# A new order of the dense work units among the attention units of a one-core transformer block

## The chip, the cores and the metric

One core of a Trainium2 chip. The time is that of the device for one execution, in microseconds (us). Engines: PE is TensorE's matmul row in the profile and PEld its weight loads, DVE is VectorE, ACT is ScalarE, SP issues the DMAs.

## The reference, cut to what matters

```python
def reference(A_x, A_wqkv, A_wo, B_x, B_w1, B_b1, B_w2, B_b2):   # bf16; S=2048, D=1024, 32 heads of 32, F=3584
    xn = layernorm(A_x)
    q, k, v = split_heads(xn @ A_wqkv)
    s = merge(softmax(q @ k.T * 32**-0.5) @ v) @ A_wo            # attention
    y = layernorm(xn)
    g = silu(gelu(y @ B_w1 + B_b1) @ B_w2 + B_b2)                # MLP, tanh form of gelu
    return A_x + s * g
```

## The kernel before

The kernel runs 512 attention units. A unit is four heads, 256 queries and 256 keys. In each turn of the main loop TensorE computes the scores of unit u, then one "dense" unit of other work, then softmax-V and row sums of unit u-1. ACT meanwhile computes the two exponentials of unit u. So dense work fills the time in which TensorE would wait for ACT.

```python
        while u < NU + LAG or state["qi"] < total or dq or act_tasks or due:
            ...
            if u < NU:
                s_unit(u)            # 8 matmuls, row tiles of 32, into 4 banks
            fill_act(u)              # tanhs that are ready may go in front of the exponentials
            if u < NU:
                exp_unit(u)          # 2 exponentials of 128x1024; the scores of u+1 reuse the banks
            ...
                else:
                    pace[:] = pg.lists["tensor"][-1:]
                    for _ in range(1 + (len(due) > 3)):     # one or two loads per unit
                        run_due()
                    pace.clear()
                if entry:
                    for s in it.steps[lo:hi]:               # the dense unit: 8 steps of 4 matmuls, or a piece of W2
                        s(state["bank"])
                    if hi == len(it.steps):
                        it.finish(state["bank"])            # DVE takes the result from the only dense bank
                if state["qi"] == q_end:                    # after the last Q/K/V unit xnT is free
                    for h in range(HG):
                        soon(NPC + 2 * h, ("wo", h), load_wo, h)
                    for t in range(NTB):
                        soon(NPC + 16, ("xres", t), load_xres, t)
                        soon(NPC + 16, ("gres", t), load_gres, t)   # transposing DMA of the gate
            if NP <= u < NU + LAG:
                pv_unit(u - LAG)     # 16 matmuls, column tiles of 32
```

A string lists the dense units in order: `a` is a W1 unit (28 per chunk of tokens, six chunks; two of them share one tanh on ACT), `q` a Q or K projection, `v` a V projection, `w3` one W2 item of 28 steps cut into 3 pieces over 3 units, `o` an output-projection unit, `.` an empty unit. Chunks have 352, 352, 320, 352, 352 and 320 tokens. Weights of W1 and W2 come from HBM anew for each chunk, in loads of 256 KB that wait in the list `due`. Two things are called gates: the gate of an output unit is g of the reference, by which DVE multiplies that unit, and the gates of W1 are the DVE steps that write the tile hT, which W2 reads.

The softmax here doesn't subtract the row's maximum and nothing guards it: scores larger than these inputs give would overflow.

Of the kernel before, what the change touches and what calls it, by code (L numbers as in the profile page):

```python
# [10 lines left out]
I32 = mybir.dt.int32  # L11

PLAN = """
q a a v a a a . a v a v a v a a a q a q a q a v q v a a a a q a a q a a q a v a q a q a q v a a q w3 w4 w3 w4 v w4 w2 w2 w2 a a v a q v v a q q a a a a a q a q a a q a a v a q a v a q a a q a a a q a a v a a q q v a a w3 q w4 w4 v w3 v q v w2 w3 w3 v w4 a v v a q q q a a a a q a a a q a a q v q a a a a v q a q a q a a a v a a q a q v q a v q a v a q a q q a w3 w3 q q q v w5 q v w4 q w3 w4 w4 w2 a a a v v a a a a q a q q v a a q a v q a q a a a a q a a a a a a q v a a a a v a v q a v q q w3 w4 w4 q w4 w4 v v w4 w3 w4 a a q q q a a a v a v a a a a a a v q a a v a a a a a a a v a q q q a a a a q q v q a v v a q w3 q w4 w4 q w4 w4 w4 w4 w4 a a a a q q a a q a a q a a a q a q a q a a a a a q a a a q a q a a a a a a q w2 w4 w3 w4 o w3 o o o o w4 o o o o o o o o o o o o w3 o o o o o o o o o o o o o w4 o o o o o o o o o o o o o . o o . o o o
"""

ENGS = ("sync", "gpsimd", "tensor", "vector", "scalar")
# [1015 lines left out]
```

## Time and profile before

The median was 1100.58 us (1100.17 to 1102.41, 3 runs).

The first part of the page of the kernel before gives busy time, its share of the span, and the number of instructions:

```profile
PE 1079.8 (98%) x29114; PEld 701.5 (64%) x29114; DVE 630.4 (57%) x1413; ACT 1043.8 (95%) x1192; POOL 20.1 (2%) x63
```

Two engines look full, so the shares do not say which one limits, and where. What tells more here is the time from one score group to the next, 503 periods from unit 8 to unit 511, sorted by the dense unit between them. The commonest values in the trace:

```
dense unit               columns streamed   period, us   period minus columns/2.4 per ns
a, q, o of 352 columns        8 x 352         2.073          0.900
a, q, o of 320 columns        8 x 320         1.966          0.899
v                             8 x 256         1.753          0.900   (smallest; median 1.781)
7-step piece of W2, 352       7 x 352         1.923          0.896
14-step piece of W2, 352     14 x 352         2.968          0.914
```

The 2.4 columns per ns are the slope of this table: 0.107 us less for 8 x 32 columns fewer, 0.320 us less for 8 x 96 fewer. At this rate the 0.90 us hold 0.64 us of columns for scores and softmax-V; the rest lies at two changes of tiling. From score start to dense start it is 0.327 us for 0.213 us of columns, and from softmax-V start to the next scores 0.542 for 0.427: 0.11 us per change. The trace does not show what the 0.11 us are made of. With these floors the 503 periods should take 1012.4 us. They took 1028.4. Only these 16 us can be won by an order.

The costs on ACT are in the groups of the kernel before (line, engine, operation, shapes, count | busy us, mean ns | idle before, with its releaser):

```profile
L858 ACT ACTIVATE P<-ps 128x1024 bf16<-128x1024 f32 x1024 | 970.3, 1077 | 16.2 <-PE ps L846 10.8
...
L846 PE MATMUL ps<-QT,KT 32*128 32x256 bf16 x4096 | 203.4, 273 | 7.4 <-ACT P L858 4.4
...
L564 ACT ACTIVATE u<-u 128x704 f32<-128x704 f32 (+1 forms) x84 | 71.0, 848 | 0.0
```

From start to start an exponential takes mostly 0.904 or 0.921 us, so a unit takes about 1.82 us of ACT. With a tanh of 704 columns between, 1.584 us pass: the tanh costs 0.68 (one of 640 columns 0.627). A V unit (1.75 us of TensorE) is shorter than the 1.82 us, and W1 units bring half a tanh each (2.16 against 2.07). There a backlog grows on ACT, and the next scores wait for their banks.

This is how it looks in the timeline of the kernel before, at a V unit whose scores started at 68.85 us (start, duration, what, [idle before and releaser]):

```profile
69.18 1.06 PE L394 MATMUL ps<-wq,xnT 128*32 128x256 bf16 x32
69.33 0.81 ACT L564 ACTIVATE u<-u 128x704 f32<-128x704 f32 x1
...
70.01 1.96 ACT L858 ACTIVATE P<-ps 128x1024 bf16<-128x1024 f32 x2
...
70.39 0.28 PE L878 MATMUL ps<-P,ones 128*32 128x256 bf16 x4
...
71.11 0.40 PE L846 MATMUL ps<-QT,KT 32*128 32x256 bf16 x8 [0.44 <-ACT P L858]
```

The tanh went first, the exponentials began at 70.01, and the next scores started at 71.11 instead of 70.60: a period of 2.26 us instead of 1.75.

The second loss sits at 960 to 990 us, where the output weights, residuals and gates load together with W2 weights. The windows view (stretch; length, then busy us and count for each engine, granted clock, DMA share, GB/s):

```profile
950.00:960.00 10.00, 10.00 (x296) 6.62 (x284) 4.38 (x12) 9.71 (x13) 0.00 (x0) 1.00 0.66 188
960.00:970.00 10.00, 10.00 (x292) 6.70 (x288) 2.09 (x4) 9.96 (x13) 0.00 (x0) 1.00 0.87 267
970.00:980.00 10.00, 8.11 (x224) 4.92 (x220) 3.37 (x8) 9.02 (x11) 0.00 (x0) 1.00 0.96 247
980.00:990.00 10.00, 9.88 (x264) 6.48 (x268) 3.02 (x8) 8.09 (x10) 0.00 (x0) 1.00 1.08 269
```

TensorE is busy for only 8.11 of the 10 us from 970. Two stops make that up. The weight loads of the first one, and the timeline of the second:

```profile
970.29 0.80 PEld L394 LDWEIGHTS ps<-hT,war 128*32 128x32 bf16 x28 [0.21 <-issue]
972.47 0.13 PEld L875 LDWEIGHTS ps<-P,VP 128*32 128x32 bf16 x4 [1.38 <-DVE trs L898]
```

```profile
978.79 0.40 PE L846 MATMUL ps<-QT,KT 32*128 32x256 bf16 x8
979.13 1.29 SPq L636 DMA_TRANSPOSE xnT<-gT_scratch  x1
979.53 0.53 DVE L665 TENSOR_TENSOR wq<-ps,xnT 128x352 f32<-128x352 f32 x1 [1.32 <-DMA xnT<-gT_scratch]
...
980.11 0.26 PEld L394 LDWEIGHTS ps<-hT,war 128*32 128x32 bf16 x12 [1.21 <-DVE wq L665]
```

The second is plain: the first output unit is finished, but DVE cannot multiply it by the gate before the gate's load lands. The only dense bank stays taken, and the next W2 piece waits. The first is put down to DVE by the view, but that transpose had ended at 971.58, and the exponentials that the softmax-V needs at 970.70. It waits for nothing that the program asks for.

### The profile page before, as it was taken

The numbers are of one execution on the slowest core, as the hardware profiler recorded it, in microseconds if no ns is written. First come the engines' busy times: TensorE is split into PE (matmuls) and PEld (weight loads), VectorE is DVE, ScalarE is ACT, GpSimd is POOL, SyncE is SP. The second block draws the span as 40 slices with busy tenths as digits, with TensorE's granted clock in tenths as the row PEclk, the third lists the DMA queues.
The fourth block names the chain that finished last, engine by engine and source line by source line (L and its number), as shares of the span: only waits on it lengthen the run. The fifth ranks groups of instructions, "written<-read, shape, count | busy, mean of one in ns | idle before, by whom it ended". The sixth has DMA issues, their size and how long they took to land.

```text
span 1099.4 us, 61736 instructions
## 1 busy us (share of the span) xinstructions
PE 1079.8 (98%) x29114; PEld 701.5 (64%) x29114; DVE 630.4 (57%) x1413; ACT 1043.8 (95%) x1192; POOL 20.1 (2%) x63
## 2 busy tenths in 40 slices
PE   7999999999999999999999999999999999999998
PEld 5766666666666666666666666666666666666665
DVE  8478853477742477642277843378732477625546
ACT  5799999899998999999999999999999999989994
POOL 2400000000000000000000000000000000000000
PEclk8999999999999999999999999999999999999999
DMA  7844447323373224342433345434244325495433
GB/s 230 164 136 148 131 112 197 92 80 109 90 179 96 72 80 132 94 103 79 132 88 118 107 100 150 119 89 127 62 114 134 90 80 147 130 263 114 105 99 108
DMA packets 209192, 131.92 MB, mean 120 GB/s; under 512 B 52522, under 2 KB 199978, under 8 KB 208938
## 3 DMA queue, kind: packets, MB, share of 16 engines
q1 hardware_dynamic: 208938, 127.97, 42.6%
q8 instruction: 228, 3.74, 1.4%
q14 instruction: 26, 0.21, 0.1%
HBM read 104.87 MB, written 12.06 MB: 106 GB/s over the span
## 4 chain that ended last, share of the span: by engine, by line
PE 54%; ACT 43%; DMA 1%; DVE 1%; SPq 0%; issue 0%; DVEq 0%
ACT P L858 39%; PE ps L394 32%; PE ps L846 9%; PE ps L875 5%; PE ps L878 5%; ACT u L564 4%; PE ps L682 1%; PE ps L698 1%; DMA xnT<-gT_scratch 0%; SPq L623 0%; ACT thz L608 0%; DMA OT<-in_A_x_dram 0%; DVE stats L322 0%; PE ps L385 0%; DVE wq L665 0%
## 5 line engine op out<-in xcount | busy, mean ns | idle before, releaser
L858 ACT ACTIVATE P<-ps 128x1024 bf16<-128x1024 f32 x1024 | 970.3, 1077 | 16.2 <-PE ps L846 10.8
L875 PE MATMUL ps<-P,VP 128*32 128x256 bf16 x4096 | 256.8, 273 | 1.3 <-ACT P L858 1.3
L878 PE MATMUL ps<-P,ones 128*32 128x256 bf16 x4096 | 256.7, 273 | 0.0
L394 PE MATMUL ps<-hT,war 128*32 128x352 bf16 (+1 forms) x5376 | 225.5, 309 | 1.0 <-DVE wq L665 0.9
L394 PE MATMUL ps<-yTc,war 128*32 128x352 bf16 (+1 forms) x5376 | 225.6, 309 | 0.2 <-issue 0.2
L846 PE MATMUL ps<-QT,KT 32*128 32x256 bf16 x4096 | 203.4, 273 | 7.4 <-ACT P L858 4.4
L394 PEld LDWEIGHTS ps<-hT,war 128*32 128x32 bf16 x5376 | 127.9, 96 | 75.4 <-issue 26.9
L394 PEld LDWEIGHTS ps<-yTc,war 128*32 128x32 bf16 x5376 | 127.6, 96 | 74.7 <-DVE xb L547 17.9
L604 DVE TENSOR_SCALAR zh<-ps,b2h 128x352 f32<-128x352 f32 (+1 forms) x48 | 27.5, 572 | 192.8 <-PE ps L394 192.8
L846 PEld LDWEIGHTS ps<-QT,KT 32*128 32x128 bf16 x4096 | 60.7, 92 | 120.2 <-issue 64.5
L547 DVE TENSOR_SCALAR xb<-ps,b1T 128x352 f32<-128x352 f32 (+1 forms) x168 | 96.2, 572 | 51.5 <-PE ps L394 47.5
L875 PEld LDWEIGHTS ps<-P,VP 128*32 128x32 bf16 x4096 | 109.8, 97 | 22.9 <-issue 1.5
L878 PEld LDWEIGHTS ps<-P,ones 128*32 128x32 bf16 x4096 | 109.9, 97 | 18.3
L570 DVE SCALAR_TENSOR_TENSOR hT<-u,xb 128x352 bf16<-128x352 f32 (+1 forms) x168 | 84.4, 509 | 63.3 <-ACT u L564 63.2
L394 PE MATMUL ps<-xnT,wq 128*32 128x352 bf16 (+1 forms) x2688 | 112.6, 309 | 0.0
L394 PEld LDWEIGHTS ps<-xnT,wq 128*32 128x32 bf16 x2688 | 63.8, 96 | 37.1 <-DVE xb L547 10.1
L557 DVE SCALAR_TENSOR_TENSOR u<-u,xb 128x352 f32<-128x352 f32 (+1 forms) x168 | 82.6, 509 | 1.6
L553 DVE TENSOR_TENSOR u<-xb 128x352 f32<-128x352 f32 (+1 forms) x168 | 82.4, 508 | 0.7
L564 ACT ACTIVATE u<-u 128x704 f32<-128x704 f32 (+1 forms) x84 | 71.0, 848 | 0.0
L394 PE MATMUL ps<-xnT,OT 128*32 128x352 bf16 (+1 forms) x1536 | 63.2, 309 | 0.2 <-DVE wq L665 0.2
L890 DVE COPY accs<-ps 128x256 f32<-128x256 f32 x64 | 26.9, 420 | 41.9 <-PE ps L878 41.8
L394 PE MATMUL ps<-wq,xnT 128*32 128x256 bf16 x1536 | 50.8, 274 | 0.0
(52 smaller groups left out, 488.4 us busy)
## 6 DMA issues: line engine op xcount, KB each, us to landing
war<-in_B_w_dram SPq DMA_DIRECT2D x336, 256.0 KB, 3.4
wq<-in_A_wqkv_dram SPq DMA_DIRECT2D x36, 128.0 KB, 2.8
OT<-in_A_x_dram SPq DMA_DIRECT2D x16, 256.0 KB, 5.2
xnT<-in_A_x_dram SPq DMA_DIRECT2D x16, 256.0 KB, 3.8
out_dram<-wq SPq DMA_DIRECT2D x16, 256.0 KB, 2.3
y_scratch<-OT SPq DMA_DIRECT2D x14, 256.0 KB, 2.5
gT_scratch<-gst SPq DMA_DIRECT2D x32, 88.0 KB, 3.2
xnT<-in_A_wo_dram SPq DMA_DIRECT2D x8, 256.0 KB, 4.5
```

What stands on the lines that cost most here:

```text
L394: ins = e.matmul(outs(j), lhsT=lhs(j), rhs=rhs, start=start, stop=stop, tile_position=(0, 32 * j), skip_group_check=True)
L547: x0 = op("vector", lambda e: e.tensor_scalar(xb[:, 0:n], bank(bk, 0, n), b1T[:, f:f + 1], None, op0=ALU.add), r=[("b", bk), "b1"], w=[kx] ...
L553: x = op("vector", lambda e: e.tensor_tensor(ub[:, 0:n], xb[:, 0:n], xb[:, 0:n], op=ALU.mult), r=[kx], w=[ku], c=151 + 1.042 * n)
L557: x = op("vector", lambda e: e.scalar_tensor_tensor(ub[:, 0:n], ub[:, 0:n], 1.0 / 0.044715, xb[:, 0:n], op0=ALU.add, op1=ALU.mult), r=[kx, ...
L564: x = op("scalar", lambda e: e.activation(ut[:, :, 0:n], ut[:, :, 0:n], ACT.Tanh, scale=0.7978845608028654 * 0.044715), r=kus, w=kus, c=48 ...
L570: op("vector", lambda e: e.scalar_tensor_tensor(hT[:, fq, 0:n], ut[:, i, 0:n], 1.0, xq[:, 0:n], op0=ALU.add, op1=ALU.mult), r=[kus[i], kq] ...
L604: x0 = op("vector", lambda e: e.tensor_scalar(zh[:, 0:n], bank(bk, 0, n), 0.25, b2h[:, nb:nb + 1], op0=ALU.mult, op1=ALU.add), r=[("b", bk ...
L846: ins = e.matmul(bank(bks[j], kh * 256, (kh + 1) * 256), lhsT=KT[i2][32 * j:32 * j + 32, k0:k0 + 128], rhs=QT[i2][32 * j:32 * j + 32, qb * ...
L858: op("scalar", lambda e, p=p, sl=sl: e.activation(pb[:, 2 * p:2 * p + 2, :, :].rearrange("p a b q -> p (a b q)"), ps[:, sl * 1024:(sl + 1) ...
L875: e.matmul(bankq(ACC, j, 0, QW), lhsT=VP[vp][:, kb, vo + 32 * j:vo + 32 * j + 32], rhs=pb[:, j, kh, :], start=first, stop=False, tile_posi ...
L878: ins = e.matmul(bankq(ACC, j, QW, 2 * QW), lhsT=ones[:, 0:32], rhs=pb[:, j, kh, :], start=False, stop=last, tile_position=(0, 32 * j), sk ...
L890: op("vector", lambda e: e.tensor_copy(a[:], bank(ACC, 0, QW)), r=[("b", ACC)], w=[ka], c=425.0)
```

## The change

Its intent, as I read it: the same units in another order, so that the tanhs of W1 meet fewer V units, and the loads of the last third are spread. Nothing else changes.

```diff
 PLAN = """
-q a a v a a a . a v a v a v a a a q a q a q a v q v a a a a q a a q a a q a v a q a q a q v a a q w3 w4 w3 w4 v w4 w2 w2 w2 a a v a q v v a q q a a a a a q a q a a q a a v a q a v a q a a q a a a q a a v a a q q v a a w3 q w4 w4 v w3 v q v w2 w3 w3 v w4 a v v a q q q a a a a q a a a q a a q v q a a a a v q a q a q a a a v a a q a q v q a v q a v a q a q q a w3 w3 q q q v w5 q v w4 q w3 w4 w4 w2 a a a v v a a a a q a q q v a a q a v q a q a a a a q a a a a a a q v a a a a v a v q a v q q w3 w4 w4 q w4 w4 v v w4 w3 w4 a a q q q a a a v a v a a a a a a v q a a v a a a a a a a v a q q q a a a a q q v q a v v a q w3 q w4 w4 q w4 w4 w4 w4 w4 a a a a q q a a q a a q a a a q a q a q a a a a a q a a a q a q a a q a a a a a a q w2 w4 w3 w4 o w3 o o o o w4 o o o o o o o o o o o o w3 o o o o o o o o o o o o o w4 o o o o o o o o o o o o o . o o . o o o
+q a a a a q a a q a q v a a a q q a a v v a a a v v a a a a a a a q v a a q v a a a a q q q w2 q v w4 w4 w2 w2 q v w2 q w4 w4 a a a a a q q a v q a a a a a v v q a q a a v a q q a v a a a a v a q a q q v a a a a a a w2 v w4 q w4 w2 w4 w4 w4 w3 a v a q a a v q q q a q v a q a a v a a q q a a q a q a v q a a a v v a a a a q q q v a q a a q a q a q v a v a q a w3 w4 q q q w4 w3 v w4 w3 w4 w3 q v a v v a a a v a a a v q a a a a q v a a v v q a a v q a a v q a a a q a q a a a v q a a a q a w3 w4 w4 w4 w4 q v q q w4 w4 w3 a a a v a q a a a q a q a q a a a v a a a a q a a v a a v q a q a a q a a q q q v v a v a a w2 q v w4 q w5 w3 q q w4 w4 w4 a a a a a q a a q a a a a a a q a q a a a q a a a q q a a q a q a a a a a w2 w4 w3 w4 w3 o o o o o o o o o o w4 o o o o o o o o o o o o w4 o o w4 o o o o o o o o o o o o o o o o o o o o o o . o o .
 """
```

Both strings hold 168 `a`, 84 `q`, 48 `v`, 48 `o` and 48 W2 items. W2 is cut into 167 instead of 166 pieces, and the empty unit near the start is gone. The last `q` is unit 439 of the dense list before and 433 after; the first `o` is 453 before and 455 after.

More of the change, by code (lines that the diff above doesn't have):

```diff
@@ L13 @@
 PLAN = """
-q a a v a a a . a v a v a v a a a q a q a q a v q v a a a a q a a q a a q a v a q a q a q v a a q w3 w4 w3 w4 v w4 w2 w2 w2 a a v a q v v a q q a a a a a q a q a a q a a v a q a v a q a a q a a a q a a v a a q q v a a w3 q w4 w4 v w3 v q v w2 w3 w3 v w4 a v v a q q q a a a a q a a a q a a q v q a a a a v q a q a q a a a v a a q a q v q a v q a v a q a q q a w3 w3 q q q v w5 q v w4 q w3 w4 w4 w2 a a a v v a a a a q a q q v a a q a v q a q a a a a q a a a a a a q v a a a a v a v q a v q q w3 w4 w4 q w4 w4 v v w4 w3 w4 a a q q q a a a v a v a a a a a a v q a a v a a a a a a a v a q q q a a a a q q v q a v v a q w3 q w4 w4 q w4 w4 w4 w4 w4 a a a a q q a a q a a q a a a q a q a q a a a a a q a a a q a q a a a a a a q w2 w4 w3 w4 o w3 o o o o w4 o o o o o o o o o o o o w3 o o o o o o o o o o o o o w4 o o o o o o o o o o o o o . o o . o o o
+q a a a a q a a q a q v a a a q q a a v v a a a v v a a a a a a a q v a a q v a a a a q q q w2 q v w4 w4 w2 w2 q v w2 q w4 w4 a a a a a q q a v q a a a a a v v q a q a a v a q q a v a a a a v a q a q q v a a a a a a w2 v w4 q w4 w2 w4 w4 w4 w3 a v a q a a v q q q a q v a q a a v a q q a a q a q a v q a a a v v a a a a q q q v a q a a q a q a q v a v a q a w3 w4 q q q w4 w3 v w4 w3 w4 w3 q v a v v a a a v a a a v q a a a a q v a a v v q a a v q a a v q a a a q a q a a a v q a a a q a w3 w4 w4 w4 w4 q v q q w4 w4 w3 a a a v a q a a a q a q a q a a a v a a a a q a a v a a v q a q a a q a a q q q v v a v a a w2 q v w4 w4 q w5 w3 q q w4 w4 w4 a a a a a q a a q a a a a a a q a q a a a q a a a q q a a q a q a a a a a w2 w4 w3 w4 w3 o o o o o o o o o o w4 o o o o o o o o o o o o w4 o o w4 o o o o o o o o o o o o o o o o o o o o o o . o o .
 """
```

## The prediction

> **What bounds the kernel now.** TensorE. The page has PE busy 98% and ACT 95% of 1099.4 us[...], so I took the start-to-start times of the 512 score groups (line 846) from the trace. Between two of them lie the softmax-V matmuls of the unit before and one dense unit. The commonest period is 2.073 us for a W1, projection or output unit of 352 columns, 1.966 for 320, 1.75 for a V unit, 1.92 for a 7-step and 2.97 for a 14-step W2 piece: each time the columns at 2.4 per ns plus 0.90 us for scores, softmax-V and two changes of tiling. The two exponentials of a unit take 1.82 us of ACT, less than 2.07; but a paired W1 tanh adds 0.68 us (exp to exp around it 1.58, not 0.90), so runs of W1 units, and W1 beside V units, turn ACT-bound.
>
> From unit 8 to 511 the periods sum to 1028.4 us; the PE floors explain about 1013. Only the excess can be won:
> - about 10 us of exponentials behind tanhs. Adding ACT work against PE floors in program order, with the durations above (an estimate), reproduces all but 14 of 503 periods within 0.06 us.
> - about 3.5 us in the burst at 960 to 990 us (DMA share 0.87 to 1.08 in the windows view): PE stops 1.2 us at 971 with no unmet dependency to be seen while its instruction fetches come late, 1.0 us at 979 because the first output unit's bank waits for the transposed gate load, and less elsewhere.
> - about 1 us of single stops.
>
> **What the change does.** It removes no work: 168 W1, 84 Q/K, 48 V, 48 output units and 48 W2 items stay, W2 in 167 pieces instead of 166; an empty unit goes. In the built program only places move. Prologue (53 us to unit 8) and tail (11 output units, 18 us after unit 511) stay.
> 1. V and Q/K units stand better between W1 units. The same sum over the new order gives an ACT excess of 4.7 us instead of 9.8: minus 5.1, mostly at V units (3.5 to 0.8).
> 2. The last Q/K/V unit comes six units earlier and the first output unit two later: 21 instead of 13 units for the loads of output weights, residuals and gates. I expect 2 to 3 of the 3.5 us back.
> 3. Against it: three chunks now go from the last W1 unit straight into a 14-step W2 piece (the one such place before had a unit between and lost 0.1 us). PE may wait there for the last gates; plus 0.3 us in all.
>
> PE being the limit, all of it is on the critical path: 1100.6 - 5.1 - 2.5 + 0.3 = about 1093.3 us; range 1090.0 to 1098.0. Faster by over 2%: 0.01; within 2%: 0.98; slower: 0.01.
>
> **What would show it.** Busy times within 1% on every engine; median periods unchanged; V units' mean period 1.84 to about 1.77; in the windows view no 10 us stretch in the last 150 us with a DMA share over 0.9, and no PE stop over 0.5 us there; waits for hT small.
>
> **What would make it wrong.** Late gates after the direct W1-to-W2 steps costing 1 to 2 us each; loads newly colliding in W2 phases, so that weights or instructions come late; score groups held by a wait that my sum leaves out.

## The result

The changed kernel took 1095.05 us (median of 4 runs, 1093.9 to 1096.37) against 1100.38 us (4 runs) beside it. The ratio is 0.995, with a 95% interval of 0.9932 to 0.9968. A later repetition gave 1094.68 us and 0.9951 (0.9937 to 0.9964).

The same lines of the page after, the busy times and the three groups:

```profile
PE 1078.7 (99%) x29114; PEld 701.8 (64%) x29114; DVE 631.4 (58%) x1413; ACT 1041.6 (95%) x1192; POOL 20.1 (2%) x63
```

```profile
L858 ACT ACTIVATE P<-ps 128x1024 bf16<-128x1024 f32 x1024 | 968.4, 1079 | 10.4 <-PE ps L846 5.4
...
L846 PE MATMUL ps<-QT,KT 32*128 32x256 bf16 x4096 | 203.3, 273 | 3.1 <-ACT P L858 0.6
...
L564 ACT ACTIVATE u<-u 128x704 f32<-128x704 f32 (+1 forms) x84 | 71.3, 853 | 0.0
```

The work is the same to 0.3%. What fell is idle time: that of PE before the scores from 7.4 to 3.1 us, that of ACT before the exponentials from 16.2 to 10.4. The waits view alone would mislead: "PEld ps L846 <- ACT P L858" is 55.3 us in 204 waits before and 52.9 us in 217 after, because the weight-load row is idle some 0.2 us ahead of nearly all scores (before, 305 more such waits, 64.5 us in all, are put down to "issue") and the view puts this down to whatever came last.

The 503 periods give the split. They took 1028.4 us before and 1022.6 after. I cut each period at the start of its dense unit and at the start of its softmax-V, and summed what lies above the usual length of each of the three parts (us, profiled executions; the last two are experiments below):

```
                          before   changed   changed, again   e1     e2
ahead of the dense unit     1.0      0.2         0.3          1.9    0.1
in the dense unit           2.5      1.4         2.0          0.9    0.4
ahead of the next scores   11.1      8.6         7.1          7.2   10.9
  of these at V units       4.2      1.2         1.2          1.3    4.1
```

The first row before was the late gate (of the 1.9 us of e1, 0.7 us are a stop of another kind). The third is mostly the wait for ACT; in the first execution of the changed kernel 1.5 us of it are stops of that other kind, shown below. So ACT waits fell from about 11 to about 7 us, of which 3 us at V units: their mean period fell from 1.841 to 1.783 us. The gate wait of 1 us is gone. But the other stops stayed. The windows view after:

```profile
940.00:950.00 10.00, 9.24 (x260) 6.02 (x254) 7.14 (x16) 9.07 (x12) 0.00 (x0) 1.00 0.80 235
950.00:960.00 10.00, 10.00 (x292) 6.66 (x288) 2.90 (x7) 10.00 (x12) 0.00 (x0) 1.00 0.87 231
960.00:970.00 10.00, 9.38 (x268) 5.93 (x261) 2.90 (x7) 8.95 (x11) 0.00 (x0) 1.00 1.01 253
970.00:980.00 10.00, 10.00 (x292) 6.73 (x292) 2.43 (x5) 9.94 (x13) 0.00 (x0) 1.00 0.94 229
```

The burst is longer and begins earlier, but it is hardly thinner: two loads are released per unit as soon as more than three wait, whatever the deadline. The timeline after, at the stop in the first of these stretches:

```profile
948.19 0.28 PE L878 MATMUL ps<-P,ones 128*32 128x256 bf16 x4
948.19 0.10 PEld L875 LDWEIGHTS ps<-P,VP 128*32 128x32 bf16 x1
...
949.12 0.29 PE L875 MATMUL ps<-P,VP 128*32 128x256 bf16 x4 [0.65 <-issue]
949.12 0.10 PEld L875 LDWEIGHTS ps<-P,VP 128*32 128x32 bf16 x3 [0.83 <-issue]
```

TensorE stopped between the first and the second of four equal weight loads of one group. No semaphore lies between them: the view says "issue". The unexplained stop of before turns out to be of the same kind. The page shows a DMA queue that it calls "instruction":

```profile
q8 instruction: 228, 3.74, 1.5%
```

228 packets of 16,384 bytes for 58,397 records of TensorE: one packet per 256 records. If TensorE's records are numbered in order of time, the stops at 972.40 us before and at 111.93, 949.12 and 963.46 us after all stand at a number that leaves 193 when divided by 256, which I call a block start. (The traces do not explain the offset of 193 itself.) There are 228 block starts too, so I pair packets and block starts in order of time; the packet of a block is called its fetch. At the four stops the packet was late: it began 2.42 to 2.46 us before TensorE went on. In quiet stretches (before, 860 to 940 us; after, 840 to 930) the packet begins with a median of 0.5 to 0.7 us after the preceding block start; in the burst of the changed kernel the median was 1.9 us, and 2.7 and 3.0 us at the two stops of 0.8 us (0.92 us less the 0.1 that lies between matmuls anyway). At the stop of before it was 3.3 us.

In these two executions (440 block starts from 54 to 1075 us) the packet began 2.40 us or more after the preceding block start in nine cases, and in all nine TensorE's records have a gap at the block start, of 0.28 to 1.27 us. Of the other 431 block starts, whose packets began at most 2.28 us after the preceding one, two have a gap of 0.24 us or more: 0.24 us at 560.81 before, which the view puts down to ACT, and 0.32 us at 102.12 after. Away from block starts these two traces have no gap of that size that the view puts down to "issue". Over all executions the border is less sharp: a few starts at 2.4 to 2.6 us had no stop, and one at 2.05 us had one.

The traces show when a packet begins, not when it was asked for, so they do not show why it was late. What they do show is that late packets and dense loads come together. For this I took all 14 profiled executions and sorted their 3088 block starts (54 to 1075 us) by the DMA share in the first 2 us of the preceding block: below 0.2 the packet begins a median of 0.3 us after the preceding block start, and none of 1129 block starts has a stop (0.24 us or more from one record to the next, with no semaphore as cause); at 0.8 and above the medians are 1.1 to 1.2 us and 30 of 533 have one, of 42 in all. Six of the 42 came at a share below 0.6, so the share does not tell everything.

### The profile page after: what moved, and what is told of

The parts are those of the page before. It is cut to its first block, busy times and chain, and to the rows that moved or that the text cites. A ratio compares the mean times of both kernels' runs of the same rounds, so it can differ in the third digit from the quotient of the medians.

```text
span 1093.2 us, 61739 instructions
## 1 busy us (share of the span) xinstructions
PE 1078.7 (99%) x29114; PEld 701.8 (64%) x29114; DVE 631.4 (58%) x1413; ACT 1041.6 (95%) x1192; POOL 20.1 (2%) x63
## 4 chain that ended last, share of the span: by engine, by line
PE 59%; ACT 40%; DVE 1%; issue 0%; DMA 0%
ACT P L858 36%; PE ps L394 35%; PE ps L846 9%; PE ps L875 6%; PE ps L878 6%; ACT u L564 3%; PE ps L682 1%; PE ps L698 1%; ACT thz L608 0%; DMA OT<-in_A_x_dram 0%; DVE stats L322 0%; ACT xnT L388 0%; PE ps L385 0%; DVE wq L665 0%; ACT VP L702 0%
## 5 line engine op out<-in xcount | busy, mean ns | idle before, releaser
L858 ACT ACTIVATE P<-ps 128x1024 bf16<-128x1024 f32 x1024 | 968.4, 1079 | 10.4 <-PE ps L846 5.4
L846 PE MATMUL ps<-QT,KT 32*128 32x256 bf16 x4096 | 203.3, 273 | 3.1 <-ACT P L858 0.6
L846 PEld LDWEIGHTS ps<-QT,KT 32*128 32x128 bf16 x4096 | 60.6, 92 | 115.0 <-issue 61.5
L394 PEld LDWEIGHTS ps<-xnT,OT 128*32 128x32 bf16 x1536 | 37.5, 96 | 19.9 <-DVE wq L665 7.7
```

The costliest lines, as they stand in the source:

```text
L394: ins = e.matmul(outs(j), lhsT=lhs(j), rhs=rhs, start=start, stop=stop, tile_position=(0, 32 * j), skip_group_check=True)
L846: ins = e.matmul(bank(bks[j], kh * 256, (kh + 1) * 256), lhsT=KT[i2][32 * j:32 * j + 32, k0:k0 + 128], rhs=QT[i2][32 * j:32 * j + 32, qb * ...
L858: op("scalar", lambda e, p=p, sl=sl: e.activation(pb[:, 2 * p:2 * p + 2, :, :].rearrange("p a b q -> p (a b q)"), ps[:, sl * 1024:(sl + 1) ...
```

## The experiments

Two pairs of theories. A: the gain is ACT backlog at V, Q/K and W1 units. B: it is the spread loads. C: the stops without a cause go with late fetches, and these with dense loads of the kernel itself. D: they are waits for data.

### e1 and e2: the new order in one part only

```diff
 # e1: first 323 dense units in the new order, the rest in the old one; e2: the reverse
-PLAN = old
+PLAN = new[units 0..322] + old[units 323..]      # e1
+PLAN = old[units 0..322] + new[units 323..]      # e2
```

At that place both orders have used up the same numbers of each kind of unit, so the halves fit.

> The new order for the first 323 dense units only, the old order after that, so the loads of the last third lie as in the kernel before. Theory A (the gain is ACT backlog that W1 tanhs no longer leave at V and Q/K units): the sum of ACT work against PE floors gives 4.9 us less for the first 323 units and nothing after, so about 1095.5 us, ratio 0.9955. Theory B (the gain is the spread loads of the last third): no gain, 1100.4 us, ratio 1.000.

> The mirror image: the old order for the first 323 units, the new one after. Theory A: the ACT excess stays at 9.6 us against 9.8, and only the stop for the first output gate (about 1 us) goes, so 1099.0 to 1100 us, ratio 0.999. Theory B: nearly the whole gain, 1095.5 us, ratio 0.9955. If A holds, this gain and that of the run before add up to that of the full change (5.3 us).

Measured: e1 1095.64 us, ratio 0.9959 (0.9947 to 0.9971); e2 1098.45 us, ratio 0.9990 (0.9977 to 1.0004), both beside 1100.25. e1 has four fifths of the gain without touching the last third, so A holds and B falls as the main cause. e2 is a small gain that its interval does not clear of zero (by its median 1.8 us, but one of its six times is 1102.41). The two shortfalls, 0.41% and 0.10%, add up to the 0.5% of the whole change. The table above shows the mechanism too: e1 takes 2.9 us off at V units and keeps the late gate (0.9 us at the same W2 piece), e2 keeps the V units and loses the gate wait.

### e3 and e4: shorter tanhs in both orders

```diff
-e.activation(ut[:, :, 0:n], ut[:, :, 0:n], ACT.Tanh, ...)
+e.activation(ut[:, :, 0:16], ut[:, :, 0:16], ACT.Tanh, ...)     # result wrong on purpose
```

> The kernel before with each W1 tanh cut to 32 of its 704 columns (the result is wrong on purpose); order of every instruction unchanged. The cost of one on ACT should fall from 0.68 to about 0.12 us (estimate: the columns' share). Theory A: the ACT excess falls from 9.8 to 1.8 us, so about 1092.4 us. Theory B: ACT is not in the way and the time stays within 2 us of 1100.4.

> The changed kernel with the same cut (wrong on purpose). Theory A: the excess falls from 4.7 to 0.2 us, so about 1090.6 us, and the distance between the two orders shrinks from 5.3 to about 2 us: 1.6 of the empty unit and V units, the rest loads. Theory B: the distance stays near 5 us.

The 0.12 us can be worked out from the two tanhs of the kernel before: 0.680 us for 704 columns and 0.627 for 640 make 0.83 ns per column, which takes 0.56 us off for 672 columns.

Measured: e3 1091.01 us (0.9917), e4 1087.19 us (0.9886), relative errors of 0.03 as intended. A tanh then cost 0.23 to 0.25 us on ACT, not 0.12. The kernel before gained 9.2 us, where A expects 8. But the distance between the orders fell only to 3.8 us, between what A and B expected, and the changed kernel gained 7.5 to 7.9 us (against its two medians) where I had expected 4.5. The traces say why the pair is not clean. The part ahead of the next scores fell from 11.1 to 2.0 us and from 7 to 0.6 us, so the backlog is real in both and I had put it 1 to 2 us too low. With ACT out of the way the old order showed new waits: about 2 us ahead of the dense unit, where DVE had not yet emptied the bank (0.3 in e4), beside one stop of 0.6 us there that waits for no semaphore, and it kept 2.0 us of stops in the dense unit (0.6 in e4). Taking one limit away shows the next one, so this pair supports A but does not measure it.

### e5 and e6: extra copies, bunched and spread

```diff
+dum = nc.dram_tensor("dum_scratch", (8 * 128, 1024), BF16).ap()
+            for i in range(8 if u in (335, 345, 400, 410, 420) else 0):                        # e5
+            for i in range(u % 8, u % 8 + (335 <= u < 355 or 400 <= u < 420)):                # e6
+                op("sync", lambda e, i=i: e.dma_start(dum[128*i:128*i+128, :], B_w1[128*i:128*i+128, 0:1024]),
+                   w=[("dum", i)], dma=f"dum{i}", after=pg.lists["tensor"][-1:])
```

Left out here: the cost that the scheduler books for a copy, and the program's wait for the copies at its very end.

> The changed kernel plus 40 copies of 256 KB from W1 to a scratch tensor that nothing reads: eight at once at units 335, 345, 400, 410 and 420, where DMA was 0.3 to 0.4 busy. Theory C [...]: each burst lasts some 8 us and so holds one or two fetches; these come over 2.2 us late and TensorE stops at the first instruction of a block, place 193 modulo 256 in the order of its records, 0.3 to 1.2 us each, 2 to 6 us in all, with no semaphore as cause. Rival D (the stops are waits for data of the loads): no stop at those places, time unchanged within 1 us, since nobody waits for these copies; at most waits for weights at other places.

> The same 40 copies, one per unit at units 335 to 354 and 400 to 419. Theory C: fetches are late by 1 us at most, no stop over 0.3 us there, time within 1 us of the changed kernel (about 1095 us). Rival D: the same. If it is slower by as much as the bursts, the bytes cost and not their bunching, and theory C falls.

The 8 us of a burst are an estimate: 2.1 MB at the 267 GB/s that the kernel before moved from 960 to 970 us.

Measured: e5 1114.13 us (ratio 1.0117), e6 1094.57 us (0.9944). The same 40 copies cost 19 us when bunched and nothing when spread: not the bytes cost, but their bunching. But the 19 us are not mainly what C expected. Weight loads in e5 (lines are numbered one higher than before), first a stop of kind C, then a wait of the dense unit, with SP's issues ahead of it:

```profile
748.14 0.86 PEld L395 LDWEIGHTS ps<-yTc,war 128*32 128x32 bf16 x25 [0.21 <-DVE xb L548]
750.92 0.12 PEld L395 LDWEIGHTS ps<-yTc,war 128*32 128x32 bf16 x7 [1.92 <-issue]
```

```profile
875.58 3.16 SPq L942 DMA_DIRECT2D dum_scratch<-in_B_w_dram  x5
878.78 2.71 SPq L503 DMA_DIRECT2D war<-in_B_w_dram  x4
```

```profile
879.02 0.39 PEld L395 LDWEIGHTS ps<-yTc,war 128*32 128x32 bf16 x16 [0.21 <-DVE xb L548]
883.97 0.14 PEld L395 LDWEIGHTS ps<-yTc,war 128*32 128x32 bf16 x8 [4.55 <-DMA war<-in_B_w_dram]
```

At 750.92 TensorE stopped for 2.0 us inside one dense unit, at a block start, though nobody reads these copies: that is C. (It lies after 25 of 32 weight loads that come in steps of four, so inside a step, and its packet had begun 4.5 us after the preceding block start.) The larger losses are weights that stood behind the copies, at units 340, 413 and 423, which D allowed for at other places: 11.7 us in six waits of the waits view. And after the two longest waits (4.6 and 4.3 us) the granted clock of the trace is 0.5 for 6.8 us each, from 881.9 and 909.2 us, and the units that followed ran slower by about 3.5 us in all (from 884.88 us four weight loads of softmax-V take 0.16 us, against 0.11 at 878). I had expected one or two stops of kind C in each burst and found one clear one in five. So a stop as C has it does come with a burst, but here the burst hurt data more: 11.7 us of waits for weights, against 2.0 us.

### e7, e10 and e11: moving the blocks under the program

```diff
             for i in range(9):
                 ins = e.matmul(bank(0), lhsT=ident[:], rhs=cold, start=True, stop=True, skip_group_check=True)
+            for i in range(64):      # e11: 32
+                ins = e.matmul(bank(0, 0, 32), lhsT=ident[:, 0:128], rhs=ident[:, 0:32], start=True, stop=True, skip_group_check=True)
             return ins
```

> The changed kernel with 64 more tiny matmuls (128 more instructions of TensorE) in the warm-up at the start, where TensorE is idle, so all later instructions move by half a block of 256. Theory C: every stop without a semaphore as cause now sits at place 193 + 128 = 65 modulo 256, and stops move to other times. Rival D: stops stay at the units where they were, at the same places in the program, whatever the block.

> The kernel of the shift run again, timed, since it had no large stop in the burst and one time of 1092.3 us. My expectation there named the wrong place: the blocks are counted from the first instruction, so they stay at 193 modulo 256 in the records, and it is the program that moves under them by 128; the one stop of that run stood at 193. If the lucky position of blocks against the burst is a lasting property of a build, the median is 1092 to 1093.5 us; if it is chance of each run, 1095 us like the changed kernel.

> The same with 32 tiny matmuls (64 instructions). Stops again only at 193 modulo 256 of the records. The time lies between 1092 and 1096 us; the spread between the three positions (0, 64 and 128 instructions) shows what position alone is worth, by theory C up to 2 us; a rival that knows only of data waits expects no difference over 0.5 us.

Measured: e7 1092.34 us in a single run, state unknown; e10, the same kernel timed, 1093.8 us (0.9939, 0.9926 to 0.9951); e11 1094.56 us (0.9947, 0.9935 to 0.9959). The expectation of e7 named the wrong place, as e10's says: the number 193 stayed and the program moved under it. The gap of 0.52 us in e7, those of 0.54 and 0.57 us in e10 and those of 0.76 and 0.43 us in e11 (each with the usual 0.1 in it) all stand at 193 and wait for no semaphore. The last one has even the same number, 51393, as the one at 963.46 us in the changed kernel, 64 instructions earlier in the program. A wait for data would have moved with the program. What the position is worth in time stays open: the three intervals overlap.

### e8: fewer loads per unit, and what it broke

```diff
-                    for _ in range(1 + (len(due) > 3)):
+                    for _ in range(1 + (len(due) > 3 and (u < 440 or u % 2 == 0))):
```

> The changed kernel with 1.5 instead of 2 loads released per unit from unit 440 on while more than three wait; order of all TensorE work unchanged. Theory C: the DMA share from 940 to 980 us falls from 0.8 to 1.0 to about 0.75, the two stops of 0.82 us there shrink to under 0.4 together, so 1 us less, 1094 us; unless loads forced at their last moment make new waits for weights, which would show as waits of the dense matmuls outside place 193. Rival D: unchanged or slower.

Measured: 1099.43 us, ratio 0.9988 (0.9974 to 1.0002): 4 us worse than the changed kernel. Up to 977 us all went as C says: DMA share 0.56 to 0.77, the latest fetch 1.3 us after its block start, no stop. But the loads now ran late. The waits view of e8:

```profile
PEld ps L394 <- DVE wq L665: 12.3, 37, 4.3
...
DVE wq L665 <- DMA xnT<-gT_scratch: 4.6, 1, 4.6
```

DVE waited 4.6 us for a gate, and the dense bank was held for that time: TensorE lost 4.0 us at the output unit that came next. It is the late gate of the kernel before, made worse. After it the granted clock is 0.5 for 3.4 us, which fits the further 1.4 us that this unit and the next lost (four matmuls of softmax-V take 0.44 us there, against 0.28 at 977). And the stops at block starts came back later: two, of 0.4 us each, at 999 and 1005 us.

### e9: fewer loads per unit, in order of their deadlines

```diff
-                        soon(NPC + 2 * h, ("wo", h), load_wo, h)
+                        soon(NPC - 1.5, ("wo", h), load_wo, h)
-                        soon(NPC + 16, ("xres", t), load_xres, t)
-                        soon(NPC + 16, ("gres", t), load_gres, t)
+                        soon(NPC - 1.4 + 0.01 * t, ("xres", t), load_xres, t)
+                        soon(NPC - 1.4 + 0.01 * t, ("gres", t), load_gres, t)
```

This stands on top of e8's edit. The last group of W2 weights, needed some 20 units later, no longer goes ahead of the first gates.

> The paced kernel of the run before, mended: still 1.5 loads per unit from unit 440 on, but output weights, residuals and gates now come before the weights of the last W2 group, which are needed only some 20 units later; the first gate is asked for at unit 459 instead of 462. TensorE's order unchanged. Theory C with the gate wait understood: the 4 us gate wait goes, the DMA share of 940 to 980 us stays at 0.75, and the stops at block starts there shrink from 1.6 us to under 0.5, so 1 to 2 us less than the changed kernel: about 1093.5 us. If stops at place 193 remain as large as in the changed kernel, pacing does not cure them; if the first output units wait for the gate again, the deadline was still missed.

> The changed kernel itself once more, five rounds, as the yardstick for the paced and reordered loads (1092.82 us, ratio 0.9935): by theory C it keeps one or two stops at place 193 in the burst of each execution and so lies at 1094 to 1096 us, ratio 0.995, with a wider scatter than the paced kernel, four of whose six times lie within 0.1 us. If it comes out at 1093 us, the paced kernel is no better.

Measured: e9 1092.82 us, ratio 0.9935 (0.9921 to 0.9948), result correct; e12 1094.68 us, ratio 0.9951 (0.9937 to 0.9964). In e9's trace no stop at a block start reaches 0.2 us anywhere after unit 8, and no gate wait is left; fetches from 937 to 992 us began at most 2.3 us after their block start. In e12's trace the stop at number 51393 was there again, 1.7 us long with the usual 0.1. The windows view of e9:

```profile
940.00:950.00 10.00, 9.85 (x288) 6.44 (x279) 6.74 (x16) 9.70 (x13) 0.00 (x0) 1.00 0.55 163
950.00:960.00 10.00, 10.00 (x292) 6.62 (x288) 2.90 (x7) 10.00 (x12) 0.00 (x0) 1.00 0.79 239
...
970.00:980.00 10.00, 10.00 (x292) 6.62 (x280) 3.07 (x6) 9.96 (x12) 0.00 (x0) 1.00 0.97 175
980.00:990.00 10.00, 10.00 (x284) 6.41 (x279) 6.56 (x16) 9.54 (x11) 0.00 (x0) 1.00 0.97 258
```

From 950 TensorE is full. The DMA share from 970 is still 0.97, not the 0.75 that I expected, so the share alone does not tell whether a fetch comes late. e9 is the fastest correct kernel by its median, among those timed more than once. Five of its six times lie between 1092.49 and 1092.90 us, while the nine times of the changed kernel lie between 1093.24 and 1096.37. The two ran on different chips, though, each beside the kernel before, and the intervals of the ratios overlap: 1.9 us less is likely, not proven. On the chip of e9, in the same rounds, e10 and e11 ran too, which are the changed kernel without pacing and with its blocks moved: e9 is only 1.0 us below the one and 1.7 below the other, and the intervals overlap there as well.

## Why the prediction was right or wrong

The time, 1095.05 us, lies in the range of 1090.0 to 1098.0, 1.8 us above the centre; a change well within 2% was foreseen. The main step was right, and one term of the sum was mis-sized.

- "Busy times within 1% on every engine; median periods unchanged": right. PE went from 1079.8 to 1078.7 us and ACT from 1043.8 to 1041.6; the periods of W1 and projection units are the same to 1 ns.
- ACT excess, "minus 5.1, mostly at V units": right in mechanism and nearly in size. The waits ahead of the scores fell from 11.1 to about 7 us, to which comes 0.6 us for the empty unit that my sum had counted here. V units gave 3 us of it (mean 1.841 to 1.783 us, foreseen 1.77). e1 alone, with the loads of the last third as before, gained 4.6 us by its medians.
- Loads, "I expect 2 to 3 of the 3.5 us back": this is the term that was mis-sized. The gate wait of 1 us went. The stops at block starts did not: in the dense units and ahead of the scores together the profiled executions hold about 2.3 us of them before, 2.7 us after and 1.9 us in the repetition. Chance has a part in it: the trace of e2, with the same last third, holds only 0.3 us of them. e2, with this part alone, is worth 0.1%, not clear of zero. I had read 21 instead of 13 units of time as a thinner burst; the loop releases two loads per unit regardless, so the share still reached 1.01. "No 10 us stretch with a DMA share over 0.9" and "no PE stop over 0.5 us there" were both wrong.
- Late gates of W1 after the direct steps into W2, "plus 0.3 us": the waits view after lists no wait of TensorE for hT in the loop. A delay of 0.2 us at one of the three places is all that the periods show there.
- "Its instruction fetches come late" was only a coincidence in time when I wrote it. The numbers 193 modulo 256, the stop inside a group of equal weight loads, and the shifted kernels tie the stops to the blocks and not to data; that the late packet is the cause is my reading of the nine cases out of nine. Why a packet is late was not shown: e5 and the sorting by DMA share show only that it goes with dense loads.

## What to carry to other kernels

When two engines are both nearly full, take the floors of one engine per work unit from the trace and add up the other's work against them in program order; that told to about 1 us what a reordering gains, where the busy shares did not move. Spread loads by their deadlines, not by releasing whatever waits: fewer loads per unit without the right order cost 4 us (e8), the same pace with deadlines gained perhaps 1 to 2 (e9). In the two main traces all ten stops of 0.24 us or more that no semaphore explains stood at block starts, multiples of 256 TensorE records apart, nine of them with a fetch that began 2.40 us or more after the preceding block start; a stop of that kind in another kernel is worth the same check.
